# Full-height, zero-padded contractions in place of packed half-height pairs in the channel mixes of a token-and-channel mixing kernel

## The chip, the cores and the metric

The kernel runs on one core of one Trainium2 chip. The metric is device time in microseconds (us) for one execution. Ratios are computed as the mean time of one kernel's runs over that of the other's of the same rounds, so they are not quite the ratios of the medians that I quote.

## The reference

Cut to what matters. The sizes are batch 8, 4224 tokens, 192 channels, 8 heads and a convolution of 7 taps.

```python
x = causal_conv_over_tokens(x, softmax(weight))        # 7 taps, 8 heads of 24 channels
theta = x @ w_theta                                    # channel mix 1: 192 x 192
zr, zi = x * cos(theta), x * sin(theta)
y = einsum('ts,bsd->btd', w_tok_r, zr) + einsum('ts,bsd->btd', w_tok_i, zi)
u = x + y                                              # the token mix is 4224 x 4224, twice
out = u + maximum(u @ w_ch, 0.0)                       # channel mix 2: 192 x 192
```

The token mixes are nearly all of the arithmetic. The change touches only the two channel mixes.

## The kernel before

It works in three passes over the input tokens, 11 chunks of 128 tokens in each. Chunk by chunk it convolves (tile `pc`), transposes (`tp`, `uT`), mixes the channels (`th`), clamps the angle (`ang`), takes cosine and sine (`zr`, `zi`) and multiplies by x. The token mix (`y`) of one pass runs while the chunks of the next are prepared. After the last pass the second channel mix (`v`) is spread over the token mix of the next row block. TensorE's order is fixed throughout by the text of the kernel. VectorE's is fixed only after the first stage, in which the first pass's chunks are prepared. ScalarE's is nowhere fixed: the framework's scheduler picks it.

192 channels are one full tile of 128 rows and a half of 64. Four batches of 128 tokens are six tiles of 128 channels. The middle tile of each three holds the last 64 channels of one batch and the first 64 of the next. The old kernel multiplies its two halves as a packed pair on the lower and upper 64 rows of the array, into two different PSUM banks:

```python
def channel_mix(dst, tT, w):            # dst: two banks; even batches in one, odd in the other
    R = D - P                           # 64
    for q in range(2):                  # two batches at a time
        v = [dst[k][:, q * D : (q + 1) * D] for k in range(2)]
        for k in range(2):              # 128 of 192 rows
            pe(nc.tensor.matmul(v[k], lhsT=tT[:, 3 * q + 2 * k, :], rhs=w[:, 2 * k, :],
                                start=True, stop=False))
        for k in range(2):              # the other 64 rows: a packed pair
            pe(nc.tensor.matmul(v[k], lhsT=tT[k * R : (k + 1) * R, 3 * q + 1, :],
                                rhs=w[k * R : (k + 1) * R, 1, :], start=False, stop=True))
```

I call these eight matmuls a block. There are 132 of them: 22 in the first stage, 44 while the second and third passes are prepared, 66 in the last pass. The first stage's loop is:

```python
for half in range(2):
    if old:
        old.theta(half)          # a block, two clamps (VectorE), cosine and sine (ScalarE)
    next(m, 0)                   # two token-mix matmuls
    if ch:
        ch.conv(2 * half)        # convolution, then its eviction xz<-pc on ScalarE
        ch.conv(2 * half + 1)
    if old:
        old.times_x()            # zr, zi times x (VectorE)
    next(m, 0)
...                              # then: load a chunk, transposes of xz on TensorE, more token mixing
```

## Time and profile before

| | |
|---|---|
| time, median of 4 runs | 1673.58 us (1673.18 to 1674.23) |
| profiled execution | 1671.0 us from first to last instruction |
| TensorE busy | 1618.1 us (97%) |
| first stage | about 121 us, everything mixed |
| the rest | about 1550 us, TensorE alone |

The page of the kernel before starts with busy time by engine (PE is TensorE, PEld its weight loads, DVE VectorE, ACT ScalarE). The last two lines are its chain of work that ended last, by engine and by line.

```profile
PE 1618.1 (97%) x8738; PEld 759.3 (45%) x8910; DVE 870.9 (52%) x1550; ACT 231.0 (14%) x366; POOL 509.7 (31%) x948
...
PE 93%; issue 1%; ACT 1%; DVE 1%; DMA 1%; SPq 0%; DVEq 0%; ACTq 0%
PE y L331 84%; PE tp L260 2%; PE v L276 2%; PE v L281 1%; PE th L276 1%; PE pc L202 1%; PE th L281 1%; DMA xs<-xz 1%; ACT xz L209 0%; ACT zi L245 0%; DVE ang L237 0%; DVE uT L264 0%; SPq L220 0%; DVE zi L251 0%; DVE pv L362 0%
```

Lines 276 and 281 are the channel mix, about 6% of the chain together. The token mix, line 331, is 84%. The table by stage says where TensorE is the limit (columns: window in us, its length, busy us and instructions of each engine, granted TensorE clock, DMA share, GB/s):

```profile
0.00:42.00 42.00, 20.84 (x138) 10.14 (x140) 25.23 (x65) 14.38 (x23) 28.92 (x61) 1.00 0.97 145
42.00:84.00 42.00, 34.59 (x277) 16.45 (x278) 28.01 (x56) 27.04 (x44) 21.77 (x40) 0.92 0.98 153
84.00:126.00 42.00, 35.20 (x246) 16.48 (x250) 27.52 (x52) 18.88 (x30) 9.41 (x17) 0.96 0.59 112
126.00:400.00 274.00, 271.89 (x1410) 126.19 (x1437) 128.05 (x225) 32.14 (x50) 89.39 (x165) 1.00 0.63 121
```

In the first 84 us the DMA engines are full and TensorE is half or four fifths busy; from 126 us on TensorE is 98 to 99% busy in every stretch, so there each nanosecond of its stream counts. One block in that stream, from the timeline of TensorE (start us, length us, then line, tiles, shape and count; runs of equal matmuls are merged):

```profile
1126.91 0.38 PE L331 MATMUL y<-zi,wt_9378 128*128 128x512 bf16 x1
1127.12 0.33 PE L276 MATMUL v<-wch,uT 128*128 128x192 bf16 x2
1127.38 0.26 PE L281 MATMUL v<-wch,uT 64*128 64x192 bf16 x2
1127.57 0.34 PE L276 MATMUL v<-wch,uT 128*128 128x192 bf16 x2
1127.84 0.26 PE L281 MATMUL v<-wch,uT 64*128 64x192 bf16 x2
1128.03 0.39 PE L331 MATMUL y<-zr,wt_9334 128*128 128x512 bf16 x1
1128.26 0.38 PE L331 MATMUL y<-zi,wt_9378 128*128 128x512 bf16 x1
```

Read the starts, not the lengths: the records overlap (a token-mix matmul is 0.38 us long, but the next starts 0.216 us after it). The block takes 0.91 us from its start (1127.12) to that of the next token-mix matmul (1128.03), whose successor comes at 0.23 us instead of the usual 0.216. The unmerged records give the gaps from start to start: 83, 178, 3, 186, 93, 178, 3, 186 ns, then 226. So the halves of a pair do run together (3 ns apart), but each passage from 128-row to 64-row matmuls or back (a change of mode, in what follows) costs about 100 ns.

### The profile page before, as it was taken

The numbers are of one execution on the slowest core, as the hardware profiler recorded it, in microseconds if no ns is written. First come the engines' busy times: TensorE is split into PE (matmuls) and PEld (weight loads), VectorE is DVE, ScalarE is ACT, GpSimd is POOL, SyncE is SP. The second block draws the span as 40 slices with busy tenths as digits, with TensorE's granted clock in tenths as the row PEclk, the third lists the DMA queues.
The fourth block names the chain that finished last, engine by engine and source line by source line (L and its number), as shares of the span: only waits on it lengthen the run. The fifth ranks groups of instructions, "written<-read, shape, count | busy, mean of one in ns | idle before, by whom it ended". The sixth has DMA issues, their size and how long they took to land.

```text
span 1671.0 us, 22525 instructions
## 1 busy us (share of the span) xinstructions
PE 1618.1 (97%) x8738; PEld 759.3 (45%) x8910; DVE 870.9 (52%) x1550; ACT 231.0 (14%) x366; POOL 509.7 (31%) x948
## 2 busy tenths in 40 slices
PE   4889999999999999999999999999999999999998
PEld 2334444444444444444444444444444444444444
DVE  5664444444444434444444444446666666666664
ACT  3640111111111001111111111101111111111111
POOL 6523333333333333333332332232222222222220
PEclk9999999999999999999999999999999999999999
DMA  9957665656566677777777776776766676667661
GB/s 145 153 109 134 126 128 108 129 120 113 119 120 107 144 175 174 164 178 161 164 177 170 161 180 166 160 172 150 169 153 165 157 162 162 160 163 163 160 160 64
DMA packets 221291, 248.36 MB, mean 149 GB/s; under 512 B 58752, under 2 KB 193920, under 8 KB 221184
## 3 DMA queue, kind: packets, MB, share of 16 engines
q0 software_dynamic: 152256, 85.24, 41.7%
q1 hardware_dynamic: 68928, 161.67, 27.0%
q8 instruction: 70, 1.15, 0.3%
q14 instruction: 37, 0.30, 0.1%
HBM read 235.27 MB, written 90.83 MB: 195 GB/s over the span
## 4 chain that ended last, share of the span: by engine, by line
PE 93%; issue 1%; ACT 1%; DVE 1%; DMA 1%; SPq 0%; DVEq 0%; ACTq 0%
PE y L331 84%; PE tp L260 2%; PE v L276 2%; PE v L281 1%; PE th L276 1%; PE pc L202 1%; PE th L281 1%; DMA xs<-xz 1%; ACT xz L209 0%; ACT zi L245 0%; DVE ang L237 0%; DVE uT L264 0%; SPq L220 0%; DVE zi L251 0%; DVE pv L362 0%
## 5 line engine op out<-in xcount | busy, mean ns | idle before, releaser
L305 POOL DMA_DIRECT2D st<-in_moe_w_tok_i_dram x396 | 212.7, 544 | 682.0 <-DVE wt_1340 L319 29.6
L305 POOL DMA_DIRECT2D st<-in_moe_w_tok_r_dram x396 | 212.7, 544 | 363.4 <-issue 18.1
L364 DVE TENSOR_TENSOR pv<-y,pv 128x512 f32<-128x512 f32 x198 | 136.6, 690 | 258.6 <-PE y L331 249.3
L362 DVE COPY pv<-y 128x512 f32<-128x512 f32 x99 | 68.2, 690 | 198.8 <-PE y L331 195.3
L264 DVE COPY uT<-tp 128x768 bf16<-128x768 bf16 x132 | 73.4, 557 | 170.0 <-PE tp L260 169.6
L242 ACT ACTIVATE zr<-ang,half_pi 128x768 bf16<-128x768 f32 x66 | 61.7, 935 | 623.6 <-DVE ang L237 623.5
L368 ACT ACTIVATE ub<-pv 128x512 bf16<-128x512 f32 x99 | 62.3, 629 | 517.4 <-DVE pv L364 517.4
L237 DVE TENSOR_SCALAR ang<-th 128x384 f32<-128x384 f32 x132 | 67.5, 551 | 78.9 <-PE th L281 78.9
L386 DVE SCALAR_TENSOR_TENSOR pv<-v,pv 128x384 f32<-128x384 f32 x132 | 67.5, 553 | 75.3 <-PE v L281 75.3
L209 ACT ACTIVATE xz<-pc 128x384 bf16<-128x384 f32 x132 | 57.7, 487 | 285.0 <-PE pc L202 169.2
L187 POOL DMA_DIRECT2D xw<-in_x_dram x132 | 76.7, 592 | 66.4 <-PE pc L202 55.3
L354 DVE TENSOR_TENSOR pv<-pv,xr 128x512 f32<-128x512 f32 x99 | 66.3, 670 | 0.0
L276 PEld LDWEIGHTS <-uT 128*128 128x128 bf16 x528 | 40.2, 98 | 43.8 <-DVE uT L264 2.1
L276 PE MATMUL th<-wth,uT 128*128 128x192 bf16 x264 | 47.2, 259 | 10.7 <-ACT xz L209 10.5
L245 ACT ACTIVATE zi<-ang 128x768 bf16<-128x768 f32 x66 | 54.7, 829 | 0.0
L202 PE MATMUL pc<-xw,bands 96*64 96x192 bf16 x528 | 38.5, 264 | 15.2 <-DMA xw<-in_x_dram 12.2
L281 PEld LDWEIGHTS <-uT 64*128 64x128 bf16 x528 | 25.4, 93 | 54.9 <-issue 54.9
L276 PE MATMUL v<-wch,uT 128*128 128x192 bf16 x264 | 44.1, 249 | 0.7 <-DVE uT L264 0.7
L202 PEld LDWEIGHTS <-bands 96*64 96x64 bf16 x528 | 22.2, 113 | 44.5 <-issue 31.4
L251 DVE TENSOR_TENSOR zr<-xz,zr 128x768 bf16<-128x768 bf16 x66 | 35.0, 530 | 9.1 <-ACT zr L242 9.0
L260 PE MATMUL tp<-ident,xz 128*128 128x128 bf16 x396 | 37.5, 233 | 2.1 <-ACT xz L209 1.8
L260 PEld LDWEIGHTS <-xz 128*128 128x128 bf16 x396 | 29.6, 105 | 21.0 <-ACT xz L209 8.3
(629 smaller groups left out, 3612.4 us busy)
## 6 DMA issues: line engine op xcount, KB each, us to landing
st<-in_moe_w_tok_r_dram POOLq DMA_DIRECT2D x396, 88.0 KB, 3.3
st<-in_moe_w_tok_i_dram POOLq DMA_DIRECT2D x396, 88.0 KB, 3.3
part_83<-pv SPq DMA_DIRECT2D x33, 768.0 KB, 3.9
pv<-part_83 SPq DMA_DIRECT2D x33, 768.0 KB, 4.3
part_84<-pv SPq DMA_DIRECT2D x33, 768.0 KB, 3.8
pv<-part_84 SPq DMA_DIRECT2D x33, 768.0 KB, 5.0
out_dram<-pv SPq DMA_DIRECT2D x66, 384.0 KB, 4.0
xs<-xz SPq DMA_DIRECT2D x132, 96.0 KB, 3.7
```

What stands on the lines that cost most here:

```text
L187: nc.gpsimd.dma_start(out=self.xw[lo : lo + n, h, :, :], in_=x[:, t0 : t0 + n, :].rearrange("b s d -> s b d"),)
L202: pe(nc.tensor.matmul(pc[half * 2 * Q : (half + 1) * 2 * Q, hh * B * G : (hh + 1) * B * G], lhsT=bands[:, h, :, :].rearrange("p a m -> p ( ...
L237: dve(nc.vector.tensor_scalar(out=every_other(ang[:, :, :], k), in0=pair(th[k]), scalar1=-CLAMP, scalar2=CLAMP, op0=ALU.max, op1=ALU.min,))
L260: pe(nc.tensor.transpose(tp[:, k * P : (k + 1) * P], u[:, k * P : (k + 1) * P], ident))
L264: dve(nc.vector.tensor_copy(out=uT[:, :, :].rearrange("p k s -> p (k s)"), in_=tp[:, 0 : 6 * P]))
L276: pe(nc.tensor.matmul(v[k], lhsT=tT[:, 3 * q + 2 * k, :], rhs=w[:, 2 * k, :], start=True, stop=False,))
L305: nc.gpsimd.dma_start(out=st[a * Q : (a + 1) * Q, :, 0 : self.ncs * Q], in_=w[self.tb * P : (self.tb + 1) * P, t0 : t0 + self.ncs * Q] .re ...
L331: pe(nc.tensor.matmul(y, lhsT=w.wt[m][:, c, :, :].rearrange("p bt i -> p (bt i)"), rhs=zs[c][m][:, cols], start=(c == 0 and m == 0), stop= ...
L354: dve(nc.vector.tensor_tensor(out=self.pv[:, cols], in0=self.pv[:, cols], in1=self.xr[:, cols], op=ALU.add,))
L362: dve(nc.vector.tensor_copy(out=pj, in_=y))
L364: dve(nc.vector.tensor_tensor(out=pj, in0=y, in1=pj, op=ALU.add))
L386: dve(nc.vector.scalar_tensor_tensor(out=pk, in0=pair(v[k]), scalar=0.0, in1=pk, op0=ALU.max, op1=ALU.add,))
```

## The change

It goes back to full-height contractions. The middle tile is multiplied whole, twice, with weights whose other half is zero. There are still eight matmuls of 192 columns a block, and none is of half height. Two neighbouring batches now share a bank, so that VectorE reads and writes 384 contiguous elements and may start after four matmuls. The diff, with cuts:

```diff
-        t = constp.tile([P, 3, D], BF16, name=name)
+        t = constp.tile([P, 4, D], BF16, name=name)
+        nc.vector.memset(t[:, 1:3, :], 0.0)
         nc.gpsimd.dma_start(out=t[:, 0, :], in_=w[0:P, :])
         nc.gpsimd.dma_start(out=t[0:R, 1, :], in_=w[P:D, :])
-        nc.gpsimd.dma_start(out=t[R:P, 1, :], in_=w[0:R, :])
-        nc.gpsimd.dma_start(out=t[:, 2, :], in_=w[R:D, :])
+        nc.gpsimd.dma_start(out=t[R:P, 2, :], in_=w[0:R, :])
+        nc.gpsimd.dma_start(out=t[:, 3, :], in_=w[R:D, :])
...
-            th = (bank("mm", "th"), bank("mm", "th"))
-            channel_mix(th, self.xT[g], wth)
-            ang = wk.tile([P, GB, D], F32, name="ang", tag="ang")
+            af = wk.tile([P, GC], F32, name="ang", tag="ang")
             for k in range(2):
                 dve(nc.vector.tensor_scalar(
-                    out=every_other(ang[:, :, :], k), in0=pair(th[k]),
+                    out=af[:, k * 2 * D : (k + 1) * 2 * D],
+                    in0=channel_mix(self.xT[g], k, wth),
...
+    def channel_mix(tT, k, w):
+        v = bank("mm", "v")
+        for b in range(2):
+            for i in range(2):
                 pe(nc.tensor.matmul(
+                    v[:, b * D : (b + 1) * D], lhsT=tT[:, 3 * k + b + i, :],
+                    rhs=w[:, 2 * b + i, :], start=(i == 0), stop=(i == 1),
                 ))
+        return v[:, 0 : 2 * D]
...                                  (the second channel mix likewise)
```

More of the change, by code (lines that the diff above doesn't have):

```diff
@@ L232, in theta @@
             cols = slice(g * GC, (g + 1) * GC)
-            th = (bank("mm", "th"), bank("mm", "th"))
-            channel_mix(th, self.xT[g], wth)
-            ang = wk.tile([P, GB, D], F32, name="ang", tag="ang")
+            af = wk.tile([P, GC], F32, name="ang", tag="ang")
             for k in range(2):
                 dve(nc.vector.tensor_scalar(
-                    out=every_other(ang[:, :, :], k), in0=pair(th[k]),
+                    out=af[:, k * 2 * D : (k + 1) * 2 * D],
+                    in0=channel_mix(self.xT[g], k, wth),
                     scalar1=-CLAMP, scalar2=CLAMP, op0=ALU.max, op1=ALU.min,
                 ))
-            af = ang[:, :, :].rearrange("p b d -> p (b d)")
             nc.scalar.activation(
@@ L267, in transposed @@
         return uT
-    def channel_mix(dst, tT, w):
-        R = D - P
-        for q in range(2):
-            v = [dst[k][:, q * D : (q + 1) * D] for k in range(2)]
-            for k in range(2):
+    def channel_mix(tT, k, w):
+        v = bank("mm", "v")
+        for b in range(2):
+            for i in range(2):
                 pe(nc.tensor.matmul(
-                    v[k], lhsT=tT[:, 3 * q + 2 * k, :], rhs=w[:, 2 * k, :],
-                    start=True, stop=False,
-                ))
-            for k in range(2):
-                pe(nc.tensor.matmul(
-                    v[k], lhsT=tT[k * R : (k + 1) * R, 3 * q + 1, :],
-                    rhs=w[k * R : (k + 1) * R, 1, :], start=False, stop=True,
-                ))
-    def pair(t):
-        return t[:, 0 : 2 * D].rearrange("p (q d) -> p q d", q=2)
-    def every_other(t, k):
-        return t.rearrange("p (q k) d -> p q k d", k=2)[:, :, k, :]
+                    v[:, b * D : (b + 1) * D], lhsT=tT[:, 3 * k + b + i, :],
+                    rhs=w[:, 2 * b + i, :], start=(i == 0), stop=(i == 1),
+                ))
+        return v[:, 0 : 2 * D]
     class Weights:
@@ L378, in output_steps @@
                 yield
-                v = (bank("mm", "v"), bank("mm", "v"))
-                channel_mix(v, uT, wch)
-                pg = self.pv[:, g * GC : (g + 1) * GC].rearrange(
-                    "p (b d) -> p b d", d=D
-                )
+                pg = self.pv[:, g * GC : (g + 1) * GC]
                 for k in range(2):
-                    pk = every_other(pg, k)
+                    pk = pg[:, k * 2 * D : (k + 1) * 2 * D]
                     dve(nc.vector.scalar_tensor_tensor(
-                        out=pk, in0=pair(v[k]), scalar=0.0, in1=pk,
+                        out=pk, in0=channel_mix(uT, k, wch), scalar=0.0, in1=pk,
                         op0=ALU.max, op1=ALU.add,
@@ L393, in output_steps @@
                     ),
-                    in_=pg,
+                    in_=pg.rearrange("p (b d) -> p b d", d=D),
                 )
```

## The prediction

> **What bounds the kernel now.** TensorE, nearly everywhere. The page has PE busy 97% of 1671.0 us and the chain that ended last runs 93% through PE, 84% of the span on the token-mixing matmuls (line 331). The table by stage gives PE 20.8, 34.6 and 35.2 us busy in the first three 42 us stretches, where DMA runs at 97%, 98% and 59%, and 98 to 99% busy in each stretch from 126 us on. So the first 126 us is mixed (DMA, ScalarE, VectorE latency); the remaining 1545 us is a stream of matmuls, where every nanosecond of PE counts. VectorE is 45 to 60% busy there, DMA 63 to 75%.
>
> **What the channel mix costs now.** 132 blocks of 8 matmuls of 192 columns: 22 in the first 126 us, 44 from there to 1128 us, 66 after. I read the starts of the matmul records around one block (timeline and chain of waits near 1127 us): full, full +83 ns, packed 64-row pair +178 ns with +3 ns between its halves, +186 to the next full one, +93, +178, +3, +186 to the next token-mixing matmul, whose successor comes 10 ns late (226 for 216). So the two packed halves do overlap (3 ns), but each change between 128-row and 64-row use costs about 100 ns. This agrees with the Trainium skill, "TensorEngine Tiling (Array Packing)", Key Properties: changing the tiling mode drains the engine. A block costs 920 ns.
>
> **After.** PE executes as many instructions in the same order. But all matmuls are now 128-row, with no mode change in the block. Full 192-column matmuls follow each other in 83 ns here, transposes with as many weight loads in 56 ns, so weight loads do not bind. The Trainium skill, "TensorE: Matmul & The Clock Gate", Back-to-back issue gap, says N/2.4 + 2.5 ns = 82.5 ns; the trace agrees (83, and 216 for 512 columns). Block: 8 x 82.5 = 660 ns. Saving 260 ns a block.
>
> **On the critical path.** 110 blocks in the PE-bound part: 110 x 0.26 = 28.6 us. At the very end VectorE can start on the first bank after four matmuls instead of eight: 0.3 us more. In the first 126 us there are 22 blocks (at most 5.7 us), but DMA is full for 84 us of it and VectorE and ScalarE latencies are on the chain; the scheduler also reorders VectorE and ScalarE a little. I count 2 us gained, give or take 3. VectorE's clamp and residual operations keep their size (384 elements, 551 and 553 ns) and are not on the path. Two memsets at the start are free. Sum: 1673.7 - 31 = 1642.7 us, just short of 2%. Range 1638.5 to 1647.0. Chances: faster by over 2% 0.22, within 2% 0.77, slower 0.01.
>
> **What the profile would show.** (1) Channel-mix matmuls start 82 to 83 ns apart, no 178 or 186 ns gaps; block 660 ns, the next token-mixing matmul at 216. (2) The chain's share of the two channel-mix lines falls from 5.8% to about 4.5%. (3) From the end of the first stage (about 126 us) to the end of the span: about 1545 becomes 1516 us. (4) First stage ends at 121 to 127 us. (5) VectorE and ScalarE busy time unchanged.
>
> **What would make it wrong.** Back-to-back accumulation into the same 192 columns at 83 ns spacing may stall (today two banks alternate); then the block is near 900 ns and nothing is gained. The first stage's reordering may cost or gain several us.

## More of the kernel before

The records of the weight loads tell a little more. Between matmuls of 128 rows, the load for the next one starts 1 to 11 ns after the start of the last. At a passage it starts only 174 to 182 ns after it, and the matmul follows within 5 ns of the load's start. So the time passes before the load; it is not the load's own 92 to 98 ns that shows.

## The result, and the profile after

| | before | after |
|---|---|---|
| time, median of 4 runs | 1673.58 us | 1645.73 us (1644.40 to 1648.79) |
| ratio | | 0.9836, 95% interval 0.9819 to 0.9853 |
| profiled execution | 1671.0 us | 1642.7 us |
| TensorE busy | 1618.1 us | 1594.7 us |

The page of the changed kernel, the same three lines (its trace has all 8910 matmul records, the old one 8738):

```profile
PE 1594.7 (97%) x8910; PEld 791.3 (48%) x8910; DVE 872.5 (53%) x1552; ACT 230.1 (14%) x366; POOL 509.6 (31%) x948
...
PE 93%; DVE 0%; ACT 0%; DVEq 0%; issue 0%
PE y L318 85%; PE v L273 4%; PE tp L259 2%; PE pc L203 1%; DVE pv L349 0%; ACT xz L210 0%; DVE pv L351 0%; ACT ub L355 0%; DVE uT L263 0%; DVE pv L369 0%; DVE zi L250 0%; DVEq L566 0%; DVEq L349 0%; DVE wt L306 0%; DVE zr L250 0%
```

The channel mix (now line 273) is 4% of the chain (4.4% unrounded; the forecast was about 4.5%), and the engines beside TensorE do what they did. The timeline of TensorE around one block of the changed kernel:

```profile
1115.55 0.38 PE L318 MATMUL y<-zi,wt 128*128 128x512 bf16 x1
1115.76 0.82 PE L273 MATMUL v<-wch,uT 128*128 128x192 bf16 x8
1116.42 0.38 PE L318 MATMUL y<-zr,wt 128*128 128x512 bf16 x1
1116.64 0.38 PE L318 MATMUL y<-zi,wt 128*128 128x512 bf16 x1
```

1115.76 to 1116.42 is 0.66 us. In the unmerged records the blocks of both later stages take 660 ns (median and mean), with gaps of 82 and 83, and the next token-mix matmul is followed at 216. So a block saves exactly the 260 ns that were forecast.

But the gain is not evenly spread. I mark the end of the first stage by the start of the first channel-mix block after it (the 23rd). It starts at 120.75 us before and at 120.84 us after. The table by stage, cut there (before at 120.76), for the kernel before:

```profile
0.00:120.76 120.76, 85.45 (x628) 40.69 (x640) 77.44 (x167) 58.63 (x95) 56.22 (x109) 0.96 0.84 135
120.76:1671.00 1550.24, 1532.69 (x8112) 718.62 (x8271) 793.50 (x1384) 172.34 (x271) 453.44 (x839) 1.00 0.68 150
```

and for the kernel after:

```profile
0.00:120.84 120.84, 78.93 (x639) 46.25 (x639) 79.37 (x169) 57.68 (x95) 56.16 (x109) 0.97 0.84 135
120.84:1642.70 1521.86, 1515.74 (x8273) 745.10 (x8271) 793.17 (x1384) 172.40 (x271) 453.48 (x839) 1.00 0.69 153
```

The rest shrank by 28.4 us (1550.24 - 1521.86). The first stage did not shrink at all, though TensorE is busy 6.5 us less in it at about the same granted clock (0.96 and 0.97, the third column from the end; 1.00 is full speed). Why not? The waits of TensorE, before:

```profile
PE tp L260 <- ACT xz L209: 1.8, 9, 0.4
```

and after (us in total, times, longest us):

```profile
PE tp L259 <- ACT xz L210: 13.3, 12, 1.7
```

The transposes of a chunk now wait 13.3 us in all for ScalarE to evict that chunk's convolution (`xz`). ScalarE's timeline in one chunk of the kernel before:

```profile
91.18 0.85 ACT L209 ACTIVATE xz<-pc 128x384 bf16<-128x384 f32 x2
93.46 0.87 ACT L209 ACTIVATE xz<-pc 128x384 bf16<-128x384 f32 x2 [1.43 <-PE pc L202]
94.22 0.94 ACT L242 ACTIVATE zr<-ang,half_pi 128x768 bf16<-128x768 f32 x1
95.04 0.84 ACT L245 ACTIVATE zi<-ang 128x768 bf16<-128x768 f32 x1
```

and of the kernel after:

```profile
91.52 0.85 ACT L210 ACTIVATE xz<-pc 128x384 bf16<-128x384 f32 x2
93.29 0.49 ACT L210 ACTIVATE xz<-pc 128x384 bf16<-128x384 f32 x1 [0.92 <-PE pc L203]
93.68 0.93 ACT L241 ACTIVATE zr<-ang,half_pi 128x768 bf16<-128x768 f32 x1
94.50 0.83 ACT L244 ACTIVATE zi<-ang 128x768 bf16<-128x768 f32 x1
95.24 0.48 ACT L210 ACTIVATE xz<-pc 128x384 bf16<-128x384 f32 x1
```

Before, all four evictions come first and the cosine and sine follow. After, the cosine and sine stand ahead of the fourth eviction, so it starts at 95.24 us, 1.56 us after the 93.68 at which they took its place behind the third. TensorE's order is the same in both programs; the listings of the two programs show that ScalarE's and, in part, VectorE's are not. Nothing in the diff names ScalarE's order: the scheduler chose another.

### The profile page after: what moved, and what is told of

It is laid out like the page before. It is cut to its first block, busy times and chain, and to the rows that moved or that the text cites. A ratio compares the mean times of both kernels' runs of the same rounds, so it can differ in the third digit from the quotient of the medians.

```text
span 1642.7 us, 22732 instructions
## 1 busy us (share of the span) xinstructions
PE 1594.7 (97%) x8910; PEld 791.3 (48%) x8910; DVE 872.5 (53%) x1552; ACT 230.1 (14%) x366; POOL 509.6 (31%) x948
## 4 chain that ended last, share of the span: by engine, by line
PE 93%; DVE 0%; ACT 0%; DVEq 0%; issue 0%
PE y L318 85%; PE v L273 4%; PE tp L259 2%; PE pc L203 1%; DVE pv L349 0%; ACT xz L210 0%; DVE pv L351 0%; ACT ub L355 0%; DVE uT L263 0%; DVE pv L369 0%; DVE zi L250 0%; DVEq L566 0%; DVEq L349 0%; DVE wt L306 0%; DVE zr L250 0%
## 5 line engine op out<-in xcount | busy, mean ns | idle before, releaser
L318 PE MATMUL y<-zi,wt 128*128 128x512 bf16 x3267 | 1239.4, 379 | 5.2 <-DVE wt L306 4.1
L318 PE MATMUL y<-zr,wt 128*128 128x512 bf16 x3267 | 1240.0, 380 | 1.9 <-DVE pv L349 1.0
L318 PEld LDWEIGHTS <-wt 128*128 128x128 bf16 x6534 | 627.9, 98 | 716.9 <-DVE wt L306 5.8
L306 DVE STREAM_TRANSPOSE wt<-st 128x512 bf16<-128x512 bf16 (+1 forms) x594 | 366.2, 644 | 0.0
L273 PEld LDWEIGHTS <-uT 128*128 128x128 bf16 x1056 | 92.8, 100 | 39.8 <-issue 9.2
L236 DVE TENSOR_SCALAR ang<-v 128x384 f32<-128x384 f32 x132 | 67.8, 550 | 55.0 <-PE v L273 54.5
L273 PE MATMUL v<-wth,uT 128*128 128x192 bf16 x528 | 59.2, 257 | 7.6 <-ACT xz L210 7.5
L273 PE MATMUL v<-wch,uT 128*128 128x192 bf16 x528 | 54.4, 246 | 0.7 <-DVE uT L263 0.7
L259 PE MATMUL tp<-ident,xz 128*128 128x128 bf16 x396 | 36.3, 228 | 13.6 <-ACT xz L210 13.3
```

Of the source, the lines that this page charges most:

```text
L236: dve(nc.vector.tensor_scalar(out=af[:, k * 2 * D : (k + 1) * 2 * D], in0=channel_mix(self.xT[g], k, wth), scalar1=-CLAMP, scalar2=CLAMP, ...
L259: pe(nc.tensor.transpose(tp[:, k * P : (k + 1) * P], u[:, k * P : (k + 1) * P], ident))
L273: pe(nc.tensor.matmul(v[:, b * D : (b + 1) * D], lhsT=tT[:, 3 * k + b + i, :], rhs=w[:, 2 * b + i, :], start=(i == 0), stop=(i == 1),))
L306: dve(nc.vector.transpose(self.wt[m][:, c:ce, :, :], self.st[m][:, :, c * Q : ce * Q].rearrange("p bt (c j) -> p c bt j", j=Q),))
L318: pe(nc.tensor.matmul(y, lhsT=w.wt[m][:, c, :, :].rearrange("p bt i -> p (bt i)"), rhs=zs[c][m][:, cols], start=(c == 0 and m == 0), stop= ...
```

## The experiments

Two theories were to be tested. Theory A: the 28 us come from the mode changes. Against it stood that they come from the banks and the contiguous access (rival B), or that a pair is slow in itself (rival C). Theory D: the first stage's share was lost to ScalarE's new order. Against it stood that DMA or the other engines bound that stage in any order (E), or that the new banks, the contiguous access or VectorE's order cost it (F). The table lists the median time, the start of the 23rd block (end of the first stage), what is left of the profiled span from there, and the granted TensorE clock of the first stage in that profile (it is 1.00 in the rest). "Old" and "new" order are the orders of ScalarE in the first stage that the old and the changed program have.

| kernel | time, us | 23rd block | rest | clock |
|---|---|---|---|---|
| before | 1673.58 | 120.75 | 1550.2 | 0.96 |
| changed | 1645.73 | 120.84 | 1521.9 | 0.97 |
| changed, again | 1646.48 | 122.94 | 1521.9 | 0.90 |
| full height, old banks (old order by itself) | 1640.85 | 117.49 | 1521.9 | 0.91 |
| changed, sines last | 1642.54 | 118.68 | 1521.7 | 0.88 |
| full height, old banks, new order | 1653.97 | 129.96 | 1521.9 | 0.88 |
| changed, old order | 1639.72 | 115.94 | 1521.7 | 0.96 |
| changed, old order, again | 1640.36 | 116.22 | 1521.6 | 0.96 |
| before with two changes a block | 1647.02 | 117.95 | 1527.0 | 0.96 |
| before with eight changes a block | 1764.55 | 148.06 | 1613.0 | 0.98 |
| packed eights, first try | 1657.35 | 117.89 | 1537.5 | 0.90 |
| packed eights, mended, on changed with old order | 1635.25 | 117.54 | 1515.8 | 0.88 |

### 1. Only the height, with everything else as before

```diff
 (old kernel, weights zero-padded as in the change)
-                    v[k], lhsT=tT[k * R : (k + 1) * R, 3 * q + 1, :],
-                    rhs=w[k * R : (k + 1) * R, 1, :], start=False, stop=True,
+                    v[k], lhsT=tT[:, 3 * q + 1, :],
+                    rhs=w[:, 1 + k, :], start=False, stop=True,
```

> The old kernel with one thing changed: the four half-height products of a block become full-height with zero-padded weights; the order of the matmuls, the alternating PSUM banks and the strided VectorE access stay. Theory A (the gain is the mode changes that go away): block 660 ns, time within 3 us of the changed kernel's 1645.7. Rival B (the gain is from one bank at a time, contiguous access or VectorE starting after four matmuls): block stays near 920 ns, time near 1673.

Measured: 1640.85 us (1639.88 to 1643.14), ratio 0.9805. The timeline of TensorE for this kernel, in which both lines of the mix now have 128 rows:

```profile
1112.42 0.33 PE L277 MATMUL v<-wch,uT 128*128 128x192 bf16 x2
1112.58 0.33 PE L282 MATMUL v<-wch,uT 128*128 128x192 bf16 x2
1112.75 0.33 PE L277 MATMUL v<-wch,uT 128*128 128x192 bf16 x2
1112.91 0.33 PE L282 MATMUL v<-wch,uT 128*128 128x192 bf16 x2
1113.08 0.38 PE L332 MATMUL y<-zr,wt 128*128 128x512 bf16 x1
```

The block takes 660 ns. Theory A holds and rival B falls: the height alone gives the whole gain of the later stages (rest 1521.9, as in the changed kernel). The time came out 4.9 us below the changed kernel's, more than the 3 us that I had allowed. All of that is in the first stage: with the old banks the scheduler kept ScalarE's old order by itself (and VectorE's), and the stage did gain 3.3 us.

### 2. Two mode changes a block

```diff
 (old kernel: four full products, then both pairs; only a bank's first matmul has start=True)
-        for q in range(2):
-            v = [dst[k][:, q * D : (q + 1) * D] for k in range(2)]
-            (two full products, then one pair)
+        for q in range(2):
+            (two full products, start=(q == 0), stop=False)
+        for q in range(2):
+            (one pair, start=False, stop=(q == 1))
```

The start flag must move because starting an accumulation clears the written-marks of a whole bank; the Trainium skill, "PSUM — Partial Sum Buffer", The four PSUM rules, says so, and also that an unmarked element is overwritten without the flag. The result was correct, which agrees.

> The old kernel with its four full products first and its two packed pairs last: two mode changes a block instead of four, nothing else. Theory A (about 100 ns for each change, a pair otherwise as cheap as one product): block with its late successor about 715 ns, time about 1673.6 - 0.2 x 110 = 1651. Rival C (not the change but the pair itself is slow, about 186 ns wherever it stands): gap from pair to pair 186, block about 815 ns, time about 1662.

Measured: 1647.02 us, ratio 0.9842. The timeline of TensorE for this kernel:

```profile
1114.73 0.38 PE L332 MATMUL y<-zi,wt 128*128 128x512 bf16 x1
1114.94 0.49 PE L276 MATMUL v<-wch,uT 128*128 128x192 bf16 x4
1115.37 0.34 PE L282 MATMUL v<-wch,uT 64*128 64x192 bf16 x4
1115.64 0.39 PE L332 MATMUL y<-zr,wt 128*128 128x512 bf16 x1
```

The block takes 697 ns and its successor is 10 late: 707, against 715 expected by theory A and 815 by rival C. Pair to pair is 89 ns where no mode changes, so a pair in itself costs about what one product costs. Two changes fewer save 920 - 707 = 213 ns: 106 ns each. The time is 4 us lower than I expected because the first stage gained 2.8 us, which I had left out, and the block 8 ns.

### 3. Eight mode changes a block

```diff
 (old kernel: each half-height product directly after its full one)
-            for k in range(2):
-                (full product of batch k)
-            for k in range(2):
-                (half product of batch k)
+            for k in range(2):
+                (full product of batch k)
+                (half product of batch k)
```

> The old kernel with full and half-height products alternating, so that nothing overlaps and the mode changes eight times a block. Theory A: all gaps in the block are 178 or 186 ns, block about 1.46 us, 0.54 us more than the old one; over 110 blocks 59 us, time about 1733. Rival C (a pair costs 186 as such, two single halves about 2 x 83): block about 0.9 to 1.0 us, time within 10 us of 1674.

Measured: 1764.55 us (two runs). The timeline of TensorE, with half of the block cut:

```profile
1197.76 0.25 PE L276 MATMUL v<-wch,uT 128*128 128x192 bf16 x1
1197.94 0.25 PE L280 MATMUL v<-wch,uT 64*128 64x192 bf16 x1
1198.12 0.26 PE L276 MATMUL v<-wch,uT 128*128 128x192 bf16 x1
...
1199.24 0.39 PE L330 MATMUL y<-zr,wt 128*128 128x512 bf16 x1
```

The block takes 1487 ns and its successor is 10 late, as theory A has it; rival C falls. Beyond the first stage it adds 62.8 us (1613.0 - 1550.2), or about 570 ns for each of 110 blocks. My total of 1733 missed because the first stage grew by 27 us, where 22 blocks account for about 13. ScalarE's order in this program is mostly of the new kind too; how much of the other 14 us is due to that was not tested.

### 4. The sines after the last eviction

```diff
 (changed kernel, first stage: theta computes its clamps and holds its cosine and sine back;
  ScalarE's instructions are chained in the order of the text)
-                    old.theta(half)
+                    old.theta(half, hold=half == 1)
                 next(m, 0)
                 if ch:
                     ch.conv(2 * half)
                     ch.conv(2 * half + 1)
                 if old:
+                    old.sine()
                     old.times_x()
```

> The changed kernel, where in the first stage alone ScalarE is held to one order: the sines of a chunk's second half after the next chunk's last eviction, as the old kernel mostly had it. The changed kernel has them before it, and its TensorE waits 13.3 us for that eviction. Theory D (the first stage gained nothing because this order gave back what the blocks saved): chunk period in the first stage falls from 8.60 us to 8.1 or less, the first stage ends 4 us earlier, time about 1641. Rival E (the first stage is bound by DMA or by VectorE and ScalarE in any order): period and time as in the changed kernel, 1645 to 1646.

Measured: 1642.54 us (1641.74 to 1643.02). The chunk period fell from 7.5 and 8.6 us to 7.0 and 7.7 in most of the later chunks, and the first stage ended at 118.68, 2.2 us earlier (at a lower granted clock, 0.88 against 0.97). This speaks for D and against E: a mere reordering frees time. It was 1.8 us less than I expected, and the order was not exactly the old one.

### 5. The changed kernel once more

Unedited, as the partner of the next ones on the same chip.

> The changed kernel itself, unedited, once more beside the next three on one chip. Every theory: about 1645.7 us, with runs from 1644 to 1649; the 22 blocks of the first stage end near 121 us in the trace.

Measured: 1646.48 us (1645.62 to 1647.01). The marker in this profile is at 122.94 us, so the first stage of this kernel differs by some 2 us from run to run; the rest does not (1521.9 both times). The granted clock of the first stage differs too: 0.97 in the first profile, 0.90 in this one. So profiles of that stage are best compared at like clocks. That the clock makes the whole 2 us was not tested.

### 6. The old banks with ScalarE's new order

```diff
 (kernel of experiment 1; after how many of a chunk's four evictions the two sine pairs stand)
+        SINES_AFTER = {1: (0, 4), 2: (0, 3), 3: (0, 3), 4: (0, 2), 5: (0, 3), 6: (1, 3),
+                       7: (1, 3), 8: (1, 3), 9: (0, 3), 10: (0, 3)}
...
+                    for n in range(2 * half, 2 * half + 2):
+                        if old and SINES_AFTER[i][half] == n:
+                            old.sine()
+                        ch.conv(n)
```

> The first experiment's kernel (full-height products in the old banks, 1640.9 us) with ScalarE in the first stage held to exactly the order that the changed kernel has (13 of its sine pairs stand elsewhere between the evictions). Theory D (the changed order of ScalarE is what costs the first stage its gain): the first stage ends near 121 us instead of 117.5, time 1644 to 1646. Rival F (the new banks, the contiguous access and VectorE's order cost it): time stays at 1640 to 1642.

Measured: 1653.97 us (1653.56 to 1654.53), ratio 0.9878, first stage to 129.96 us. TensorE waits 15.2 us for the evictions, where experiment 1 has 2.1. So the new banks and the contiguous access are not needed for the loss, and that part of rival F falls. Its third part does not: the trace shows that VectorE's order, which was left free, moved here to one much like the changed kernel's. The direction is theory D's, but the size is not: 13 us instead of 4. Why the new order costs the old banks twice what it costs the new ones (next experiment) was not tested.

### 7. The new banks with ScalarE's old order

```diff
 (changed kernel, as in 6, with)
+        SINES_AFTER = {1: (0, 4), 2: (0, 4), 3: (0, 4), 4: (1, 4), 5: (0, 4), 6: (2, 4),
+                       7: (2, 4), 8: (0, 4), 9: (0, 4), 10: (0, 4)}
```

> The changed kernel with ScalarE in the first stage held to exactly the order that the old kernel has; banks, contiguous access and all matmuls as in the changed kernel. Theory D: the first stage ends near 118 us, time 1640.5 to 1643. Rival F: time stays at 1644 to 1647.

Measured: 1639.72 us (1639.30 to 1641.00), ratio 0.9794, 6.8 us below the changed kernel of the same job and 0.8 us below the range that I had given. The wait of TensorE for the last eviction is back to what it was:

```profile
PE tp L271 <- ACT xz L214: 1.8, 9, 0.4
```

Every matmul, bank and access of the change is in this kernel, and its first stage ends at 115.94 us. The changed kernel's two profiles have 122.94 at a clock of 0.90 and 120.84 at 0.97; the clock here is 0.96, so the fair difference is 4.9 us. The whole times agree: the three runs of each program with a mean clock of 0.996 took 1645.48 to 1646.45 us with the new order (experiment 5 and the first result) and 1639.30 to 1639.64 with the old one (this experiment and 9). So the clock does not explain the difference, and theory D is shown, with one limit: VectorE's order in the first stage was left to the scheduler and mostly followed ScalarE's, so the two are not separated.

### 8. Packing eight batches, first try

If two changes cost 213 ns, and each pair replaces two products with one (83 ns saved), then packing should pay once three pairs share one visit to the half-height mode (3 x 83 = 249). After the first stage two blocks were merged: eight full products, then four pairs, in four banks.

```diff
 (kernel of experiment 1, after the first stage)
+    def packed_mix(dsts, tTs, w):
+        for dst, tT in zip(dsts, tTs):
+            (four full products, start=(q == 0), stop=False)
+        for dst, tT in zip(dsts, tTs):
+            (two pairs, start=False, stop=(q == 1))
```

A variant with neighbouring batches in one bank was not run: both row halves would then write one bank unordered. The Trainium skill, "TensorEngine Tiling (Array Packing)", Gotcha 1: PSUM Pressure, says the same; no run here shows it.

> An attempt to beat both: the first experiment's kernel, where after the first stage two blocks become one of 8 full products followed by 4 packed 64-row pairs, so that two mode changes are paid for eight batches and the packing's saving is kept. From the gaps of the two-change run (83, 178, 3, 89, 175, successor 10 late) the double block should take 1.22 us instead of 1.32; 55 of them give 5.3 us, time about 1635.5. Rival G (four PSUM banks filled at once make the stream wait for VectorE): time 1641 or more.

Measured: 1657.35 us. The double block took 1192 ns and 10 late, even less than forecast, yet the kernel lost 16.5 us. The waits of TensorE show where:

```profile
PE tp L262 <- ACT ub L391: 16.4, 33, 1.3
```

It was not the reason that I had written down, four banks at once (rival G). In merging I had moved the second transposes of each row block to the place directly after the block's last sum, where ScalarE has not yet rounded that sum (`ub`): half a microsecond of waiting, 33 times. By the starts of the matmuls it is more, 22 us in all, since the wait is counted from modelled ends. The tail after the start of the last block grew from 5.7 us (experiment 1) to 7.7 us as well.

### 9. The partner of the last run

> The changed kernel with the old ScalarE order, unedited from its last run, once more as the partner of the next one on the same chip: 1639 to 1641 us.

Measured: 1640.36 us (1639.64 to 1640.50).

### 10. Packing eight batches, mended

```diff
 (kernel of experiment 7 with packed_mix after the first stage)
             for g in range(NG):
                 uTs.append(transposed(self.ub[:, g * GC : (g + 1) * GC]))
                 yield
+                if g == 0:
+                    yield            # the second transposes stay where they were
...
+            if self.tb == NT - 1:
+                yield from self.single_steps()      # last row block: unpacked
```

> The packed double block again, now on the changed kernel with the old ScalarE order. Two faults of the failed try are mended: the second transposes of a row block go back to their old place (there they waited 16.4 us in all for ScalarE), and the last row block is done in the unpacked way. The failed try's own double blocks took 1.20 us where two unpacked ones take 1.32. If only misplacement made it fail, 54 double blocks save 6.4 us: about 1633.5 us, and TensorE's wait for the eviction of ub is gone. If four banks filled at once hold the stream up (theory G), 1638 or more.

Measured: 1635.25 us (1634.94 to 1637.43), ratio 0.9771 to the kernel before, 5.1 us below its partner. The timeline of TensorE:

```profile
1131.73 0.38 PE L356 MATMUL y<-zi,wt 128*128 128x512 bf16 x1
1131.94 0.82 PE L298 MATMUL v<-wch,uT 128*128 128x192 bf16 x8
1132.70 0.50 PE L306 MATMUL v<-wch,uT 64*128 64x192 bf16 x8
1133.13 0.39 PE L356 MATMUL y<-zr,wt 128*128 128x512 bf16 x1
```

16 matmuls in 1.19 us, against 1.32 for two unpacked blocks. The rest shrank from 1521.6 to 1515.8 us, 5.8 of the 6.4 expected. The first stage, in which the two kernels have the same text and the same orders of ScalarE and VectorE, was 1.3 us longer in this profile, at a granted clock of 0.88 instead of 0.96. Theory G falls, and this version beats both kernels.

## Why the prediction was right or wrong

The measured 1645.73 us lies in the range of 1638.5 to 1647.0, 3 us above the point, and "within 2%" came true. Point by point:

- **Mode changes bound the block: right, and shown.** 920 ns became 660 as forecast. Experiments 1 to 3 have no, two and eight changes instead of four, and one account fits them all: 83 ns for each product or packed pair, and about 106 ns for each change. (The 106 was read from the difference between four changes and two, so eight changes and the double block are its tests.) Four changes: 6 x 83 + 4 x 106 = 922 (920 measured). Two: 6 x 83 + 2 x 106 = 710 (707). Eight, nothing packed: 8 x 83 + 8 x 106 = 1512 (1497). A double block with four pairs: 12 x 83 + 2 x 106 = 1208 (1202). A part that the change leaves alone shows gaps of the same size: in both kernels the convolution's matmuls on 64 columns of the array (96\*64 in the profile), also packed in pairs, start 310 ns after the token-mix matmul before them instead of 216, the token mix starts 178 ns after their last one, and its successor comes 10 ns late.
- **Stalls from accumulating in one bank at 83 ns: feared, not found.** The blocks after the first stage take 660 ns on average too, not only in the median.
- **28.6 us in the later part: right.** 28.4 us were measured for it and the end together. **The 0.3 us at the very end: not shown.** VectorE does start 0.61 us after the start of the last block, where the old banks have 0.86 (experiment 1). But the rest of the two kernels differs by only 0.04 us, and between the changed kernel and that of experiment 7, whose later stages are the same, it differs by 0.2.
- **The step that was mis-sized is "I count 2 us gained" in the first 126 us.** The measured gain was -0.1 us in one profile and -2.2 in the other. The prediction named the danger ("the scheduler also reorders VectorE and ScalarE a little") but took it for small. It costs 6.8 us in the medians (experiment 7 against 5), 4.9 us between profiles of like clock. Without it the first stage gains about 4.5 to 4.8 us, most of the 5.7 that I had called the most it could be; so the full DMA queues and the latencies of the other engines, my reasons for counting only 2 us, held back little. The total came within 3 us because the mis-sized term was a small one.
- **Other engines unchanged: right** (VectorE 870.9 to 872.5 us, ScalarE 231.0 to 230.1). Busy time said nothing of the loss: the same instructions in another order cost it.

What stays open is why the scheduler chose another order, how much of the cost is VectorE's part of it, and why it weighs double on the old banks. Whether the new banks help by themselves is not settled either: with the old order, the changed kernel took 1639.72 and 1640.36 us, experiment 1 took 1640.85, and its profile has the lower clock in the first stage (0.91 against 0.96).

## What to carry to other kernels

Packing half-height matmuls pays only if enough pairs share one visit to that mode: here a visit cost 213 ns and a pair saved 83, so two pairs lose and four win (three were not run); count changes of mode, not only rows in use. When a change leaves some engine's order to a scheduler, compare the built order on every engine, also on those that the diff does not name, and look for work that has moved ahead of the instruction that the bottleneck waits for. A saving on the busiest engine can be given back in the one stage where that engine is not the limit, so read the gain stage by stage.

## What the Trainium skill lacked or had wrong

- "TensorEngine Tiling (Array Packing)", Key Properties, says that changing the tiling mode drains TensorE but gives no size: about 106 ns for each change between 128-row and 64-row matmuls of 192 columns here. No page says that a weight load is not brought forward across such a change; here it started 174 to 182 ns after the last matmul's start instead of 1 to 11. That page's table Theoretical Speedup promises up to 2x for contractions of 64 or less and has no break-even: with one pair a visit, packing lost 260 ns in a block of 920.
- "TensorE: Matmul & The Clock Gate", Back-to-back issue gap, gives for real kernels, with their weight loads, about 81 ns a matmul at 128 columns and 131 at 512. Here, with a weight load before each, it was 56 and 216 ns, and 83 at 192 columns. Its formula for the isolated matmul, N/2.4 + 2.5, fits all three.
- The same page, Part 3, The mechanism, says in its list of what overlaps that a weight load runs beside a matmul only when its row group differs, and just before it that a background weight buffer does as well. The second is what fits here: weight loads of 98 ns over all 128 rows ran beside matmuls over all 128 rows: products with a load each followed at 83 ns, transposes at 56.
- Its span model, about 4 ns between packed matmuls, agrees (3 ns here).
